# Score products moved ahead in the early slots, two maxima per even slot at the hand-over, and a new order of the tail, in a kernel of threshold attention followed by a gated two-layer product

## The chip, the cores and the metric

The kernel runs on one core of one Trainium2 chip. A core has five engines that work at the same time, each in the order of its own queue: TensorE (PE, matrix products and transposes through the array), VectorE (DVE), ScalarE (ACT), GpSimd (POOL) and SyncE (SP, which here only starts DMAs). The metric is the time of one execution in device microseconds; lower is better.

## What is computed

Eight batches of eight heads, 576 positions, head dimension 64. Scores within tau of the row's maximum stay, all others are dropped; what is left goes through a softmax and is multiplied with v. The result, as 4608 tokens of 512 features, goes through two products with an activation between them.

```python
scores = scale * np.matmul(q, k.transpose(0, 1, 3, 2))
thresh = np.max(scores, axis=-1, keepdims=True) - tau
scores = np.where(scores >= thresh, scores, -1000000000.0)
scores = scores - np.max(scores, axis=-1, keepdims=True)
attn = np.exp(scores)
attn = attn / (np.sum(attn, axis=-1, keepdims=True) + 1e-09)
return np.matmul(attn, v).astype(np.float32)
...
h = x @ w_in
relu6 = np.clip(h + 3.0, 0.0, 6.0)
g = h * relu6 / 6.0
return (g @ w_out).astype(np.float32)
```

## The kernel before

**Slots.** Four heads make a quad (two pairs), and a quad has nine slots. Slots 0 to 3 are the four blocks of 128 query rows of the first pair, 4 to 7 those of the second, and slot 8 takes the 64 rows left over of both pairs. A slot holds the scores of two heads, 128 rows by 576 keys each. There are 16 quads and so 144 slots, which one loop goes through (L518); `now` is the number of the slot in hand. The order of the instructions on every engine is written out by hand, and there is no scheduler: an engine does what its queue says in the order in which the loop recorded it.

**One slot's way through the engines.** `scores(n)` (L287, PE) writes the scores to PSUM. `sm_max` (L302, DVE) copies them to the tile `s` and takes the row maximum of each head; its last line (L305, POOL) makes the bias from it. `sm_mask` (L309, ACT) rejects what is below the threshold, `sm_exp` (L314, ACT) takes the exponential and the row sum. `sm_recip` (L317, DVE) inverts the sum, `sm_norm` (L322, POOL) multiplies and writes `pn` in bf16, to be transposed into `pT` (or `pR` for slot 8): for most slots up to 20 by PE (`pe_transpose`, L337, and a DVE copy L338), for all others by a DMA that SP starts (L330). In iteration n the loop takes the maxima of slot n+1, the mask and exp around slot n, the norm of slot n-1, the transposition of slot n-2, and the scores of slot n+2.

**Products.** `products` says after which slot `av_main` (L346, L349) multiplies pT with v into `xT`, and `av_rest` does so with pR into `xR`. The DVE copies them out of PSUM (L357, L367).

**q and k.** They have to be transposed: for the first two batches by PE (L232, L257, L259; `turns` says in which slot) with a copy by DVE or ACT (L239, L220, L222, L265), later by DVE itself. `loads` are closures that start the loads of q and k, on SP for the first two batches and partly on POOL (kr) later; one or none is started in each slot. `casts` and `vcasts` do the same for the weights and for v, on POOL.

**The two layers.** An item of `todo1` is one first-layer product: `mm1` (L381, or L376 for the odd tokens, the 64 rows of slot 8 in two batches), the activation `mm1_relu` (on ACT in even slots, L389, on DVE in odd ones, L391) and the gate `mm1_gate` (L404, DVE). Items of the odd tokens write their gate to `go`, of which there is one buffer, and a DMA transposes it into `g` (L406). A token tile of `todo2` is the second-layer product of 128 tokens, 16 matmuls in four pieces (`mm2_part`, L415), and `mm2_out` (L421 on ACT, L423 on DVE) copies it out for the final DMA. There are no items before slot 22 (`N1`); from there each slot takes one item, and two pieces of a tile go into every even slot once there are tiles.

**PSUM.** It has eight banks. Scores take banks 0, 1, 3 and 4 (in odd slots after 24 another set of columns, reaching into 2 and 5), transposes and products take turns in 2 and 5 (`bank()`), bank 6 (`HB`) holds PE's transposed pn, dummy transposes and the items, bank 7 (`OB`) the token tile or an item.

**Dummy transposes.** `warm_up(6)` puts six transposes of the identity on PE in each of the first eight slots.

**Tail.** After the loop come the last products, the items left over, the norm of the last slot, the first eight items of the last batch (`head`), the rest of the products (`av_rest` needs pR of slot 143), the tiles in hand, then the twelve last items (`tail`), and the last three tiles. In the tail items take banks 0, 1, 3 and 4 in turn, tiles take banks 7 and 6.

Of the kernel before, what the change touches and what calls it, by code (L numbers as in the profile page):

```python
# [20 lines left out]
def kernel(  # L21
# [17 lines left out]
    NQUAD = B * H // 4  # L39
    NSLOT = 9  # L40
    NB = 2
    N1 = 22
    N2 = 28
    HB, OB = 6, 7
# [171 lines left out]


    def copy_out(out, in_):
        if 0 <= now < N1:
            nc.vector.tensor_copy(out=out, in_=in_)  # L220
        else:
            nc.scalar.copy(out=out, in_=in_)  # L222
# [54 lines left out]
    def scores(n):  # L277
        quad, slot = divmod(n, NSLOT)
        w0 = 320 if first(n) else 384
        for k0, w in ((0, w0), (w0, S - w0)):  # L280
            for i in range(2 if slot == 8 else 1):
                for a in range(2):
                    pair = 2 * quad + (i if slot == 8 else slot // 4)
                    rows = slice(64 * i, 64 * i + 64) if slot == 8 else slice(0, P)
                    q0 = 512 if slot == 8 else slot % 4 * P
                    c0, kc = score_col(n, a) + k0, 64 * (1 - a) + k0
                    nc.tensor.matmul(ps_flat[rows, c0:c0 + w],  # L287
                                     qT_of(pair)[a * 64:(a + 1) * 64, q0:q0 + rows.stop - rows.start],
                                     kT_of(pair)[a * 64:(a + 1) * 64, kc:kc + w], start=True, stop=True)
# [4 lines left out]
    def sm_max(sl):  # L294
        sl.s = s_pool.tile([P, 2, S], F32, tag="s", name="s")
        sl.m = stat_pool.tile([P, 2], F32, tag="m", name="m")
        sl.bias = stat_pool.tile([P, 2], F32, tag="bias", name="bias")
        sl.rsum = stat_pool.tile([P, 2], F32, tag="rsum", name="rsum")
        sl.rinv = stat_pool.tile([P, 2], F32, tag="rinv", name="rinv")
        for i in range(2):  # L300
            c0 = score_col(sl.n, i)
            nc.vector.tensor_scalar(out=sl.s[:, i, :], in0=ps_flat[:, c0:c0 + S],  # L302
                                    scalar1=1.0, scalar2=None, op0=Alu.mult, op1=Alu.max,
                                    accum_out=sl.m[:, i:i + 1])
        nc.gpsimd.tensor_scalar(out=sl.bias[:], in0=sl.m[:], scalar1=-scale, scalar2=tau, op0=Alu.mult, op1=Alu.add)  # L305

    def sm_mask(sl, i):
# [8 lines left out]
    def sm_recip(sl):  # L316
        nc.vector.reciprocal(out=sl.rinv[:], in_=sl.rsum[:])  # L317
# [122 lines left out]
    def moe_of(b):  # L440
        items = []
        for c0, mts in (((0, (5, 6)), (None, (4,)), (256, (7, 8))) if b % 2 else ((0, (0, 1)), (256, (2, 3)))):
            for ni in range(0, NI, 4 if c0 is None else 2):
                items.append(((b, ni, c0), ()))
            items[-1] = (items[-1][0], [(b // 2, mt, part) for mt in mts for part in range(4)])
        if b % 2:
            items[10:14] = items[12:14] + items[10:12]
        return items[0:8], items[8:]

    alloc_qk(0)  # L450
# [24 lines left out]
            queue.append(sl)  # L475
    scores(0)
    sm_max(queue[0])
    scores(1)

    turns = {1: [("q", 1)], 2: [("k", 1)], 3: [("rest", 0)]}  # L480

    def turn_at(n, job, of):
        turns.setdefault(n, []).append((job, of))

    for quad in range(1, NQUAD):
        n0 = quad * NSLOT
        first_odd = n0 - 9 + quad % 2
        for i, (job, of) in enumerate((("q", 2 * quad), ("k", 2 * quad), ("rest", quad),
                                       ("q", 2 * quad + 1), ("k", 2 * quad + 1))):
            turn_at(n0 + (-5, -4, -3, 0, 1)[i] if quad < 3 else  # L490
                    first_odd + (0, 2, 3, 4, 6)[i] if quad > 3 else first_odd + (0, 2, 3, 5, 7)[i], job, of)

    products = {}
    for quad in range(NQUAD):
        p0, p1 = 2 * quad, 2 * quad + 1
        if quad < NB:
            jobs = ((8, p0, 0, 512), (12, p1, 0, 512), (13, None, 0, 0))
        else:
            jobs = [(7 - quad % 2 + 2 * i, *of) for i, of in enumerate(
                ((p0, 0, 256), (p0, 256, 256), (p1, 0, 256), (p1, 256, 256), (None, 0, 0)))]  # L500
        for after, *of in jobs:
            products.setdefault(quad * NSLOT + after, []).append((quad, *of))

    def multiply(n):
# [6 lines left out]
                todo1.extend(moe_of(of // 2)[0])  # L511
        return copies

    prev = None
    last_keys = []
    part = 0
    waiting = []
    for n, sl in enumerate(queue):  # L518
        quad, slot = sl.quad, sl.slot
        b, g = divmod(quad, 2)  # L520
        now = n
        if slot in (0, 4):
            pts[2 * quad + slot // 4] = pt_pool.tile([P, 9, 512], BF16, tag="pT", name="pT")
        if slot == 8:
            ptr[quad] = ptr_pool.tile([P, 9, P], BF16, tag="pR", name="pR")
        for ahead in {0: (1, 2), 9: (3,), 16: (4,)}.get(n, (quad + 2,) if quad > 2 and slot == (2 if quad == 3 else 0) else ()):
            if ahead < NQUAD:
                load_quad(ahead)
        if slot == 0 and g == 1 and b + 1 < B:
            load_v(b + 1)  # L530
        for copy in last_keys:
            copy()
        last_keys = []
        if 0 < n <= N1:
            for i in range(2):
                sm_exp(prev, i)
        if n + 1 < len(queue):
            sm_max(queue[n + 1])
        even = n >= N1 and n % 2 == 0
        if n > N1:  # L540
            sm_recip(prev)
        for copy in waiting:
            copy()
        waiting = []

        if todo1:
            item, then = todo1.pop(0)
            h = mm1(item, OB if n > N1 and n % 2 and not pieces else HB)
            todo2.extend(then)
        else:  # L550
            item = None
        if n >= N1:
            for copy in multiply(n):
                copy()
        if item:
            mm1_gate(item, h, mm1_relu(h, on_act=even))
        copies = pe_transpose(queue[n - 2]) if n > 1 and queue[n - 2].on_chip else None
        if prev is not None and n < N1:
            sm_recip(prev)
        if copies:  # L560
            copies()
        pieces = 2 if n % 2 == 0 and todo2 else 0
        for _ in range(pieces):
            bb, mt, part = todo2.pop(0)
            mm2_part(bb, mt, part)
        if n <= N1:
            for i in range(2):
                sm_mask(sl, i)
        if n == N1:
            sm_recip(prev)  # L570
        if n >= N1:
            for i in range(2):
                sm_exp(sl, i)
            if n + 1 < len(queue):
                for i in range(2):
                    sm_mask(queue[n + 1], i)
        if n < N1:
            for copy in multiply(n):
                copy()
        if part == 3:  # L580
            waiting.append(lambda tile=(bb, mt): late.extend(mm2_out(*tile, on_act=False)))
            part = 0
        evict = []
        for job, of in turns.get(n, ()):
            if job == "k":
                (last_keys if even else evict).append(transpose_k(of))
            elif job == "q":
                if of // 2 not in qkT:
                    alloc_qk(of // 2)
                (waiting if even else evict).append(transpose_q(of))  # L590
            else:
                (last_keys if even else evict).append(transpose_rest(of, of_k=of > 0))
        for out_of_psum in evict:
            if out_of_psum:
                out_of_psum()
        if n == 0:
            warm_up(8)
        if n <= N1:
            scores(n + 2)
        elif n % 2:  # L600
            for m in (n + 3, n + 2):
                if m < len(queue):
                    scores(m)
        if n < 8:
            warm_up(6)
        if n > 0:
            sm_norm(prev)
        flush()
        if n == 0:
            start(loads, 2)  # L610
        elif n not in (4, 12, 15, 18, 21) and not 23 < n < 30 and (n < 37 or n % 2 == 0):
            start(loads, 1)
        if n < 4 or 15 < n < 20 or n > 33:
            start(vcasts, 1 if n < N1 or n % 2 else 0)
        else:
            start(casts, 2 if n in (5, 8, 11, 14) or 21 < n < 28 else 1)
        prev = sl
# [34 lines left out]
    sm_recip(prev)  # L652
    sm_norm(prev)
    head, tail = moe_of(B - 1)
    for item in head:
        rest1(*item)
    av_main(2 * last + 1, 256, 256)()
    av_rest(last)()
    rest2()
# [38 lines left out]
```

## Time and profile before

| what | value |
|---|---|
| median of 13 runs | 522.2 us (521.39 to 524.29) |
| the profiled execution | 522.2 us |
| its span, first to last instruction | 520.4 us |
| granted clock of TensorE | 1.00 |
| busy: PE, ACT, DVE, POOL | 506.3, 452.0, 442.4, 299.3 us |

```profile
L309 ACT ACTIVATE s<-s,bias 128x576 f32<-128x576 f32 x288 | 205.9, 763 | 6.0 <-POOL bias L305 5.7
L314 ACT ACTIVATE s<-s 128x576 f32<-128x576 f32 x288 | 192.6, 671 | 0.3
L287 PE MATMUL ps<-kT,qT 64*128 64x384 f32 (+7 forms) x1280 | 174.0, 419 | 4.7 <-DVE s L302 3.8
```

A row of the page's costliest groups names the line, the engine and the operation, what it writes and reads, how often, then the busy time and the mean length of one in ns, then how long the engine stood idle ahead of it and what ended most of that. The whole execution falls into a start, slots 0 to 21 with attention alone (to about 76 us), slots 22 to 143 with both (to about 468 us), and the tail. An engine's share of the whole span says little about any of these, so the readings below go by stage.

### The profile page before, as it was taken

To read this page: it belongs to the slowest core of one execution; us is meant where nothing else is said; L and a number is where in the kernel's file an instruction comes from. 1 tells how busy PE (TensorE), PEld (TensorE's weight loads), DVE (VectorE), ACT (ScalarE), POOL (GpSimd) and SP (SyncE) were. 2 spreads that over 40 slices of the span, in tenths; PEclk is the share of its full clock that TensorE was granted. 3 is DMA by queue.
4 is the path that set the end of the run, shared out by engine and by line. 5 is a ranking of instruction groups with operands and counts; after the bars stand their busy time and mean duration, and the time that the engine had idled before them with its cause. 6 is when DMAs were issued, how large, how long until landed. Compare 5 with 4: busy or idle time off the path is not lost.

```text
span 520.4 us, 12124 instructions
## 1 busy us (share of the span) xinstructions
PE 506.3 (97%) x4145; PEld 321.4 (62%) x4145; DVE 442.4 (85%) x1124; ACT 452.0 (87%) x980; POOL 299.3 (58%) x538
## 2 busy tenths in 40 slices
PE   8999999999999999999999999999999999999997
PEld 6765556666665666666665666666655666667463
DVE  3788887998999999999999999999999999878151
ACT  3999979999999989999999999999999999995060
POOL 1778869756676655657566656657566655551000
PEclk9999999999999999999999999999999999999999
DMA  5899899989899999999989999999999996574222
GB/s 131 118 174 166 143 158 143 195 142 170 153 167 180 164 179 167 175 162 170 175 160 173 172 184 160 160 172 171 159 157 189 181 172 113 112 112 70 83 61 60
DMA packets 314094, 78.77 MB, mean 151 GB/s; under 512 B 296624, under 2 KB 309168, under 8 KB 314032
## 3 DMA queue, kind: packets, MB, share of 16 engines
q1 hardware_dynamic: 294464, 67.90, 77.0%
q0 software_dynamic: 18368, 9.71, 15.1%
q8 instruction: 32, 0.52, 0.4%
q10 hardware_dynamic: 1200, 0.39, 0.3%
q14 instruction: 30, 0.25, 0.1%
HBM read 36.70 MB, written 9.44 MB: 89 GB/s over the span
## 4 chain that ended last, share of the span: by engine, by line
PE 76%; ACT 3%; DMA 2%; DVE 2%; issue 1%; POOL 1%; POOLq 0%; DVEq 0%
PE ps L287 24%; PE ps L415 23%; PE ps L381 19%; PE ps L346 6%; PE ps L376 2%; ACT s L309 1%; PE ps L349 1%; ACT s L314 1%; DMA pT<-pn 1%; ACT r L389 1%; DVE s L302 1%; DMA pR<-pn 1%; POOL pn L322 1%; DVE g L404 1%; DMA g<-go 1%
## 5 line engine op out<-in xcount | busy, mean ns | idle before, releaser
L322 POOL TENSOR_SCALAR pn<-s,rinv 128x576 bf16<-128x576 f32 x288 | 210.6, 743 | 18.7 <-issue 4.4
L302 DVE TENSOR_SCALAR_CACHE_REDUCE s<-ps 128x576 f32<-128x576 f32 x288 | 205.1, 749 | 17.5 <-PE ps L287 9.0
L309 ACT ACTIVATE s<-s,bias 128x576 f32<-128x576 f32 x288 | 205.9, 763 | 6.0 <-POOL bias L305 5.7
L314 ACT ACTIVATE s<-s 128x576 f32<-128x576 f32 x288 | 192.6, 671 | 0.3
L287 PE MATMUL ps<-kT,qT 64*128 64x384 f32 (+7 forms) x1280 | 174.0, 419 | 4.7 <-DVE s L302 3.8
L287 PEld LDWEIGHTS ps<-kT,qT 64*128 64x128 f32 (+1 forms) x1280 | 103.6, 175 | 59.3 <-issue 15.8
L415 PE MATMUL ps<-w_out_sb,g 128*128 128x512 bf16 x576 | 134.0, 379 | 0.0
L381 PE MATMUL ps<-xT,w_in_sb 128*128 128x256 bf16 x1024 | 130.8, 273 | 1.2 <-DVE g L404 0.7
L381 PEld LDWEIGHTS <-w_in_sb 128*128 128x128 bf16 x1024 | 95.5, 98 | 41.0 <-issue 22.2
L305 POOL TENSOR_SCALAR bias<-m 128x2 f32<-128x2 f32 x144 | 26.9, 187 | 155.6 <-DVE rinv L317 138.7
L404 DVE SCALAR_TENSOR_TENSOR g<-r,ps 128x512 bf16<-128x512 f32 x128 | 87.6, 687 | 9.6 <-ACT r L389 5.6
L415 PEld LDWEIGHTS <-g 128*128 128x128 bf16 x576 | 56.3, 98 | 56.6
L389 ACT ACTIVATE r<-ps,three 128x512 f32<-128x512 f32 x81 | 55.4, 687 | 29.4 <-PE ps L381 21.8
L314 ACT ACTIVATION_READ_ACCUMULATOR s<-s 128x1 f32 x288 | 54.6, 190 | 0.0
L391 DVE TENSOR_SCALAR r<-ps 128x512 f32<-128x512 f32 x63 | 42.9, 681 | 0.0
L346 PE MATMUL ps<-pT,vm 128*64 128x256 bf16 (+1 forms) x480 | 39.1, 285 | 0.5 <-DMA pT<-pn 0.5
L346 PEld LDWEIGHTS <-vm 128*64 128x64 bf16 x736 | 27.2, 110 | 17.0 <-issue 14.8
L357 DVE CAST xT<-ps 128x256 bf16<-128x256 f32 (+1 forms) x60 | 26.3, 438 | 13.2 <-PE ps L349 13.2
L423 DVE TENSOR_SCALAR osb<-ps 128x512 f32<-128x512 f32 x31 | 20.9, 673 | 13.1 <-PE ps L415 13.1
L302 DVE DVE_READ_ACCUMULATOR s<-ps 128x1 f32 x288 | 23.9, 83 | 0.0
L317 DVE RECIPROCAL rinv<-rsum 128x2 f32<-128x2 f32 x144 | 23.0, 160 | 0.6 <-ACT s L314 0.6
L143 POOL DMA_DIRECT2D vm<-in_v_dram x28 | 21.4, 765 | 0.7 <-issue 0.7
(57 smaller groups left out, 259.9 us busy)
## 6 DMA issues: line engine op xcount, KB each, us to landing
out_dram<-osb SPq DMA_DIRECT2D x31, 256.0 KB, 3.0
nq<-in_q_dram SPq DMA_DIRECT2D x96, 72.0 KB, 3.7
km<-in_k_dram SPq DMA_DIRECT2D x96, 64.0 KB, 3.2
vm<-in_v_dram POOLq DMA_DIRECT2D x24, 128.0 KB, 4.4
km<-in_k_dram SPq DMA_DIRECT2D x16, 128.0 KB, 4.2
w_in_sb<-in_moe_w_in_dram POOLq DMA_DIRECT2D x16, 128.0 KB, 3.9
w_out_sb<-in_moe_w_out_dram POOLq DMA_DIRECT2D x16, 128.0 KB, 4.8
pT<-pn SPq DMA_TRANSPOSE x117, 4.1
```

The costliest lines, as they stand in the source:

```text
L287: nc.tensor.matmul(ps_flat[rows, c0:c0 + w], qT_of(pair)[a * 64:(a + 1) * 64, q0:q0 + rows.stop - rows.start], kT_of(pair)[a * 64:(a + 1) ...
L302: nc.vector.tensor_scalar(out=sl.s[:, i, :], in0=ps_flat[:, c0:c0 + S], scalar1=1.0, scalar2=None, op0=Alu.mult, op1=Alu.max, accum_out=sl ...
L305: nc.gpsimd.tensor_scalar(out=sl.bias[:], in0=sl.m[:], scalar1=-scale, scalar2=tau, op0=Alu.mult, op1=Alu.add)
L309: nc.scalar.activation(out=s, in_=s, func=Act.Prelu, bias=sl.bias[:, i:i + 1], scale=scale, alpha=REJECT)
L314: nc.scalar.activation(out=s, in_=s, func=Act.Exp, accum_out=sl.rsum[:, i:i + 1])
L322: nc.gpsimd.tensor_scalar(out=pn[:, i, :], in0=sl.s[:, i, :], scalar1=sl.rinv[:, i:i + 1], scalar2=1.0, op0=Alu.mult, op1=Alu.mult)
L346: nc.tensor.matmul(pb[a * 64:(a + 1) * 64, :], vm[:, 2 * hp + a, c * D:(c + 1) * D], pT[:, 5 * a + c, cols], start=(c == 0), stop=False)
L381: nc.tensor.matmul(ps[:, hb, n * 256:(n + 1) * 256], w_in_sb[:, ki, (ni + n) * P:(ni + n + 1) * P], xT[b][:, ki, c0:c0 + 256], start=(ki = ...
L389: nc.scalar.activation(out=r, in_=hps, func=Act.Relu, bias=three[:])
L391: nc.vector.tensor_scalar(out=r, in0=hps, scalar1=3.0, scalar2=0.0, op0=Alu.add, op1=Alu.max)
L404: nc.vector.scalar_tensor_tensor(out=out, in0=r, scalar=6.0, in1=hps, op0=Alu.min, op1=Alu.mult)
L415: nc.tensor.matmul(o_ps[0], gbuf[:, ni, mt * P:(mt + 1) * P], w_out_sb[:, ni, :], start=(ni == 0), stop=(ni == NI - 1))
```

## The change

It has two parts.

**The tail.** The odd tokens' second two items of the last batch come after four other items instead of after two (`items[10:16]`). In slot 142 the two pieces of the token tile are recorded ahead of the item's product. The item of slot 143 uses bank 0. After the loop, the tiles in hand are taken between the seventh and the eighth item of `head`, ahead of the last products.

**The slots up to 28.** In slots 3 to 22 (`N0` to `N1`) `scores(n + 2)` is recorded right after the maxima and the reciprocal, ahead of PE's transposes and products; the copies of these are kept in `waiting` and recorded in the next slot, behind its maxima and its reciprocal. The slots in which q and k of quads 1 and 2 are transposed, and in which products of quads 0 and 1 are taken, are moved, five loads instead of two are started in slot 0, and dummy transposes are left in slots 0, 1, 2, 3 and 6. The bias is a function of its own (`sm_bias`). In the even slots from 22 to 28 the maxima of slots n+1 and n+2 are both taken, ahead of the item's gate, and none in the odd slots between. There exp comes ahead of the item's activation, and in slot 22 both masks (22 and 23) do too.

```diff
--- before.py
+++ after.py
@@ -39,6 +39,7 @@
     NQUAD = B * H // 4
     NSLOT = 9
     NB = 2
+    N0 = 3
     N1 = 22
     N2 = 28
     HB, OB = 6, 7
@@ -216,7 +217,7 @@
 
 
     def copy_out(out, in_):
-        if 0 <= now < N1:
+        if 0 <= now <= N1:
             nc.vector.tensor_copy(out=out, in_=in_)
         else:
             nc.scalar.copy(out=out, in_=in_)
@@ -302,6 +303,8 @@
             nc.vector.tensor_scalar(out=sl.s[:, i, :], in0=ps_flat[:, c0:c0 + S],
                                     scalar1=1.0, scalar2=None, op0=Alu.mult, op1=Alu.max,
                                     accum_out=sl.m[:, i:i + 1])
+
+    def sm_bias(sl):
         nc.gpsimd.tensor_scalar(out=sl.bias[:], in0=sl.m[:], scalar1=-scale, scalar2=tau, op0=Alu.mult, op1=Alu.add)
 
     def sm_mask(sl, i):
@@ -443,8 +446,10 @@
             for ni in range(0, NI, 4 if c0 is None else 2):
                 items.append(((b, ni, c0), ()))
             items[-1] = (items[-1][0], [(b // 2, mt, part) for mt in mts for part in range(4)])
-        if b % 2:
+        if b % 2 and b < B - 1:
             items[10:14] = items[12:14] + items[10:12]
+        elif b % 2:
+            items[10:16] = items[12:16] + items[10:12]
         return items[0:8], items[8:]
 
     alloc_qk(0)
@@ -475,6 +480,7 @@
             queue.append(sl)
     scores(0)
     sm_max(queue[0])
+    sm_bias(queue[0])
     scores(1)
 
     turns = {1: [("q", 1)], 2: [("k", 1)], 3: [("rest", 0)]}
@@ -487,14 +493,14 @@
         first_odd = n0 - 9 + quad % 2
         for i, (job, of) in enumerate((("q", 2 * quad), ("k", 2 * quad), ("rest", quad),
                                        ("q", 2 * quad + 1), ("k", 2 * quad + 1))):
-            turn_at(n0 + (-5, -4, -3, 0, 1)[i] if quad < 3 else
+            turn_at(n0 + ((-5, -5, -4, -2, -1) if quad == 1 else (-6, -5, -4, -2, -1))[i] if quad < 3 else
                     first_odd + (0, 2, 3, 4, 6)[i] if quad > 3 else first_odd + (0, 2, 3, 5, 7)[i], job, of)
 
     products = {}
     for quad in range(NQUAD):
         p0, p1 = 2 * quad, 2 * quad + 1
         if quad < NB:
-            jobs = ((8, p0, 0, 512), (12, p1, 0, 512), (13, None, 0, 0))
+            jobs = ((8, p0, 0, 512), (13 - 2 * quad, p1, 0, 512), (15 - 3 * quad, None, 0, 0))
         else:
             jobs = [(7 - quad % 2 + 2 * i, *of) for i, of in enumerate(
                 ((p0, 0, 256), (p0, 256, 256), (p1, 0, 256), (p1, 256, 256), (None, 0, 0)))]
@@ -511,9 +517,16 @@
                 todo1.extend(moe_of(of // 2)[0])
         return copies
 
+    def second():
+        nonlocal pieces, bb, mt, part
+        pieces = 2 if now % 2 == 0 and todo2 else 0
+        for _ in range(pieces):
+            bb, mt, part = todo2.pop(0)
+            mm2_part(bb, mt, part)
+
     prev = None
     last_keys = []
-    part = 0
+    pieces = bb = mt = part = 0
     waiting = []
     for n, sl in enumerate(queue):
         quad, slot = sl.quad, sl.slot
@@ -535,17 +548,37 @@
             for i in range(2):
                 sm_exp(prev, i)
         if n + 1 < len(queue):
-            sm_max(queue[n + 1])
+            if n <= N1 or n > N2 + 1 or n % 2 == 0:
+                sm_max(queue[n + 1])
+            sm_bias(queue[n + 1])
         even = n >= N1 and n % 2 == 0
-        if n > N1:
+        if n >= N0:
             sm_recip(prev)
         for copy in waiting:
             copy()
         waiting = []
-
-        if todo1:
+        if N0 <= n <= N1:
+            scores(n + 2)
+            if n in (3, 6):
+                warm_up(6)
+        if even and n <= N2:
+            sm_max(queue[n + 2])
+        if n == N1:
+            for i in range(2):
+                sm_mask(sl, i)
+        exp_first = even and n <= N2
+        if exp_first:
+            for i in range(2):
+                sm_exp(sl, i)
+        if n == N1:
+            for i in range(2):
+                sm_mask(queue[n + 1], i)
+
+        if todo1 and n >= N1:
             item, then = todo1.pop(0)
-            h = mm1(item, OB if n > N1 and n % 2 and not pieces else HB)
+            if n == len(queue) - 2:
+                second()
+            h = mm1(item, 0 if n == len(queue) - 1 else OB if n > N1 and n % 2 and not pieces else HB)
             todo2.extend(then)
         else:
             item = None
@@ -554,29 +587,27 @@
                 copy()
         if item:
             mm1_gate(item, h, mm1_relu(h, on_act=even))
-        copies = pe_transpose(queue[n - 2]) if n > 1 and queue[n - 2].on_chip else None
-        if prev is not None and n < N1:
+        if n > 1 and queue[n - 2].on_chip:
+            waiting.append(pe_transpose(queue[n - 2]))
+        if prev is not None and n < N0:
             sm_recip(prev)
-        if copies:
-            copies()
-        pieces = 2 if n % 2 == 0 and todo2 else 0
-        for _ in range(pieces):
-            bb, mt, part = todo2.pop(0)
-            mm2_part(bb, mt, part)
-        if n <= N1:
+            for copy in waiting:
+                copy()
+            waiting = []
+        if n != len(queue) - 2:
+            second()
+        if n < N1:
             for i in range(2):
                 sm_mask(sl, i)
-        if n == N1:
-            sm_recip(prev)
         if n >= N1:
-            for i in range(2):
-                sm_exp(sl, i)
-            if n + 1 < len(queue):
+            if not exp_first:
+                for i in range(2):
+                    sm_exp(sl, i)
+            if n != N1 and n + 1 < len(queue):
                 for i in range(2):
                     sm_mask(queue[n + 1], i)
         if n < N1:
-            for copy in multiply(n):
-                copy()
+            waiting.extend(multiply(n))
         if part == 3:
             waiting.append(lambda tile=(bb, mt): late.extend(mm2_out(*tile, on_act=False)))
             part = 0
@@ -590,24 +621,26 @@
                 (waiting if even else evict).append(transpose_q(of))
             else:
                 (last_keys if even else evict).append(transpose_rest(of, of_k=of > 0))
+        evict = [out_of_psum for out_of_psum in evict if out_of_psum]
+        if N0 <= n < N1:
+            waiting.extend(evict)
+            evict = []
         for out_of_psum in evict:
-            if out_of_psum:
-                out_of_psum()
+            out_of_psum()
         if n == 0:
             warm_up(8)
-        if n <= N1:
+        if n < N0:
             scores(n + 2)
-        elif n % 2:
+            warm_up(6)
+        elif n > N1 and n % 2:
             for m in (n + 3, n + 2):
                 if m < len(queue):
                     scores(m)
-        if n < 8:
-            warm_up(6)
         if n > 0:
             sm_norm(prev)
         flush()
         if n == 0:
-            start(loads, 2)
+            start(loads, 5)
         elif n not in (4, 12, 15, 18, 21) and not 23 < n < 30 and (n < 37 or n % 2 == 0):
             start(loads, 1)
         if n < 4 or 15 < n < 20 or n > 33:
@@ -652,8 +685,10 @@
     sm_recip(prev)
     sm_norm(prev)
     head, tail = moe_of(B - 1)
-    for item in head:
+    for item in head[0:7]:
         rest1(*item)
+    rest2()
+    rest1(*head[7])
     av_main(2 * last + 1, 256, 256)()
     av_rest(last)()
     rest2()
```

## The prediction

> **What bounds the kernel now.** I read the page's busy shares first, then busy time by stage, then the waits of each engine, then the timeline. The profiled execution took 522.2 us, of which the span is 520.4; the median of the 13 runs is 522.2 too, so a sum made on the span may be taken off the median.
>
> ```profile
> PE 506.3 (97%) x4145; PEld 321.4 (62%) x4145; DVE 442.4 (85%) x1124; ACT 452.0 (87%) x980; POOL 299.3 (58%) x538
> 21.46:70.12 48.66, 45.79 (x375) 29.22 (x374) 41.97 (x117) 46.39 (x103) 39.70 (x72) 1.00 1.03 167
> 70.12:76.12 6.00, 5.73 (x51) 3.31 (x51) 4.78 (x12) 2.77 (x6) 4.19 (x7) 1.00 0.90 112
> 80.70:102.46 21.76, 19.60 (x154) 13.79 (x152) 18.63 (x49) 21.67 (x49) 18.78 (x35) 1.00 1.28 184
> 102.46:458.90 356.44, 355.96 (x2992) 223.43 (x2990) 333.60 (x850) 336.82 (x741) 218.87 (x388) 1.00 1.02 164
> ```
>
> In the rows by stage the figures are length, then busy time of PE, PE loads, DVE, ACT, POOL, then clock. From 102.5 to 458.9 us PE is the bound (355.96 of 356.44). From 80.7 to 102.5 it is ACT (21.67 of 21.76). Slots 4 to 21 (21.46 to 70.12) are ACT's as well, nearly: it is idle for 2.27 us. Then, in slot 22, it stands still for 3.2 us:
>
> ```profile
> ACT s L309 <- POOL bias L305: 2.3, 5, 0.6
> ACT r L389 <- PE ps L381: 3.2, 1, 3.2
> 75.03 1.05 PE L381 MATMUL ps<-xT,w_in_sb 128*128 128x256 bf16 x8
> 76.12 0.69 ACT L389 ACTIVATE r<-ps,three 128x512 f32<-128x512 f32 x1 [3.23 <-PE ps L381]
> 76.70 1.43 ACT L309 ACTIVATE s<-s,bias 128x576 f32<-128x576 f32 x2
> ```
>
> ACT's first hidden-layer activation sits in its queue ahead of slot 22's mask, and waits for a projection that PE reaches only after scores(23). The third place is the end, where PE waits:
>
> ```profile
> PE ps L381 <- DVE g L404: 0.7, 1, 0.7
> PE ps L381 <- DVE go L404: 0.6, 1, 0.6
> PE ps L346 <- DMA pR<-pn: 0.3, 1, 0.3
> ```
>
> The steady stage is not touched by the diff, so all that can change lies before 102.5 and after 458.9. Work saved in the first part arrives at the end in full, because PE then starts its 356 us earlier.
>
> **What the Trainium skill says.** "Perfetto Trace Analysis", section "Tensor Engine Instruction", says that ACT, DVE and GpSimd work strictly in the order of their queues and that the end of a matmul is modelled. The 3.23 us wait agrees: slot 22's bias was ready at 72.6 us (POOL wrote it at 72.45) and its mask stood behind the activation until 76.7. "TensorE: Matmul & The Clock Gate", section "What's actually happening", says that TensorE falls to half its clock after an idle window of about 3.4 us. No stage of the trace shows it: slots 8 to 21 have no dummy transposes, and the granted clock is 1.00 in all of them.
>
> **The change part by part.**
>
> Slots 3 to 21. Moved: scores(n+2) goes ahead of PE's pn transposes, products and q/k transposes, and the copies of these go behind the maxima of the next slot. Nothing is added; the same instructions run. The question is what the cycle costs each engine. ACT: two exps and two masks; mask starts at 15.64 and 18.30, 24.14 and 26.81 give 2.67 us a slot without a wait. Seventeen slots are 45.4 us, against 48.66 now, so 3.3 us is the most to gain (2.27 by the busy column, whose overlapping durations hide small gaps).
>
> DVE and PE: the maxima need scores, scores need the maxima before them to be through.
>
> ```profile
> 10.99 0.76 DVE L302 TENSOR_SCALAR_CACHE_REDUCE s<-ps 128x576 f32<-128x576 f32 x1 [1.02 <-PE ps L287]
> 13.49 0.76 DVE L302 TENSOR_SCALAR_CACHE_REDUCE s<-ps 128x576 f32<-128x576 f32 x1 [1.05 <-PE ps L287]
> 26.39 0.74 DVE L338 COPY pT<-ps 128x1152 bf16<-128x1152 bf16 x1
> 27.05 0.68 DVE L220 COPY kT<-ps 128x512 f32<-128x512 f32 x1
> 28.05 0.76 DVE L302 TENSOR_SCALAR_CACHE_REDUCE s<-ps 128x576 f32<-128x576 f32 x1 [0.32 <-issue]
> ```
>
> The first two rows, 2.50 us apart, are that cycle with no copies. With copies DVE needs 1.36 for two maxima, 0.07 for the reciprocal, 0.66 for a pT copy, about 0.68 for a q, k or xT copy, 0.86 for the three small ones of a rest. The third to fifth rows show such a slot, and 0.32 us lost at its end since the scores came after the copies. With scores first, a slot costs the larger of 2.50 and 1.43 plus its copies. By the new order, slots 4 to 20 have: 2.50, 2.79, 2.95, 2.50, 2.77, 2.80, 2.50, 2.50, 2.50, 2.77, 2.80, 2.95, 2.50, 2.77, 2.80, 2.50, 2.77. The sum is 45.7, and it runs ahead of or behind ACT's 2.67 by at most 0.4 us on the way. So DVE and ACT are now equal, and ACT loses some 0.4 us more. A PE slot with a product (scores to 1.2 us after the maxima, product 1.43, q or k transposes 0.6, sum 3.2) is late by 0.5 us, but the slot after it has 1.37 us of copies ahead of the next maxima, which hides it. Gain between 0 (any 0.2 us more in each DVE slot takes it all) and 2.9; I take 2.6.
>
> POOL: bias 0.2, two norms 1.47, weight loads 0.57 or 1.12 make 2.3 to 2.85 us a slot; slots 5, 8, 11, 14 have the 2.85, within what DVE gives. The loads of quad 1 all start in slot 0: three more closures, four pairs of DMAs of some 1.25 us each on SP, 5.0 us. SP is free from 9.8 us and its first transposing DMA is issued at 16.80, so they fit, and quad 1's data is there by slot 4 (they land in 3 to 4 us). Quad 4's last load comes in slot 20 instead of 22: 1.28 us more on POOL there, which holds bias(22) back by about 0.8. Three of the eight sets of dummy transposes after slot 3 go: nothing, since PE has real work there; if the clock did fall to half, slots 4 to 7 would need some 4.8 us instead of 2.67, 8.5 us in all.
>
> Slot 22. On ACT, mask(22), exp(22) and mask(23) now stand ahead of the activation: three pairs, 4.0 us, which need only bias(22) and max(23). max(23) no longer waits for copies of its own slot. The 3.23 us go. What is late next is the same activation: PE does scores(24) (1.24) once max(23) ends, 2.4 us after exp(21), then the projection (1.05); with latencies and PE's leftover work the activation can start 4.95 us after exp(21). ACT is there at 4.0, and held back by bias(22) at 4.8, both inside the same wait. 0.95 is given back: gain 2.3, between 1.3 and 3.2.
>
> Slots 23 to 28. Both maxima of a pair of slots are now taken in the even one, ahead of the gate, and exp goes ahead of the activation. ACT is already 99.6% busy here with the same instructions, so nothing to gain by itself: 0. Below: the gate of an even slot stands behind max(n+2), which waits for scores(n+2). I place the gate of slot 22 at 6.2 us after exp(21), and PE wants that bank for slot 24 at 8.7, a margin of 2.5. Above: PE is idle 2.16 us in this stage, and scores that are released sooner could let it enter the steady stage with a longer lead, up to 1.5.
>
> Loop end. In slot 142 two pieces of the token tile (1.73 us) go ahead of the projection, which waited 0.66 for a gate. The projection and its activation come 1.05 later, ACT's exp(142) with them, and recip(142), which stands ahead of the xT copy on DVE, ends at 468.6, where that copy started before. So DVE keeps its absolute times, and PE, 0.66 earlier, meets them four banks later: gate of the second leftover item at 473.4, wanted at 473.0. Of 0.66 I count 0.1.
>
> Tail. The leftover tiles (ten pieces, 8.7 us) go between the seventh and eighth items of the last batch and so ahead of the products with pR: its 0.28 us wait goes, covered by 8.7. The second pair of odd items comes six after the first: the first transposing DMA took 3.5 us with its wait, four items of 0.9 us now lie in it, so the 0.57 goes. The second transposition lands about 12.0 us after the tail's start, and is wanted at 12.3: nothing, with 0.3 to spare. 0.85 together.
>
> Sum: 2.6 + 2.3 + 0 + 0.1 + 0.85 = 5.85, so 522.2 - 5.85 = 516.4 (rounded up).
>
> **The rivals.**
>
> DVE's cycle doesn't shorten. The scores come sooner, but reciprocal, late copies and reads of PSUM keep slots at 2.8 us; for it speaks that my DVE sum equals ACT's. Then only slot 22 and the end remain: 2.3 + 0.95 = 3.25, 519.0.
>
> The lead counts. PE's idle 2.16 us in slots 23 to 28 shrinks too, by 1.5: 514.9. For it speaks that PE's long matmul rows there (2.88 against 2.2 us in the steady stage) contain waits; against it, that ACT is full.
>
> Slower: the gate behind the second maxima. In slots 22, 24, 26 and 28 DVE stands at max(n+2) until PE has done scores(n+2), the gate is late, its bank holds the projection two slots on, and ACT's activation waits with all masks behind it. It decides from a lateness of 2.5 us on. At 1.9 us lost by ACT in each of four slots, 7.6: 516.4 + 7.6 = 524.0; below 1.46 each the change is still a gain.
>
> **How the numbers follow.** Forecast 0.55 (515.4 to 517.8), DVE's cycle 0.20 (517.8 to 521), the lead 0.15 (513.6 to 515.4), the gates 0.10. The range 514.4 to 519.8 leaves out the slower case and the ends of two others. About 0.2%, 1 us, is what this kernel's runs can tell from no change: faster 0.86, no change 0.05, slower 0.09.
>
> **What would show it.** ACT's wait for the first activation falls from 3.2 to about 1 us; that activation stands after slot 23's mask; the masks of slots 4 to 21 are 2.7 us apart; the steady stage begins near 97.5 instead of 102.5 and is as long as before; the waits for pR and go are absent. The prediction is wrong if masks stay 2.85 apart, if new waits of ACT appear between slots 22 and 30, or if PE's clock drops below 1.00 before slot 8.

## The result, and the profile after

The changed kernel took 517.0 us (median of 7 runs, 516.42 to 517.45) against 522.31 us before (32 runs); the ratio is 0.9894 with a 95% interval of 0.9882 to 0.9907. The prediction said 516.4. The profiled execution has a span of 514.8 us, 5.6 us less than before.

These are rows of busy time by stage, of the changed kernel, in the columns used before (length, then busy time of PE, PE loads, DVE, ACT, POOL, then clock, DMA share and GB/s). The stages end at the mask of slot 21, at ACT's copies of k in slot 23, at the first piece of a token tile, and at the activation of slot 140.

```profile
21.30:67.94 46.64, 45.04 (x355) 27.59 (x355) 40.78 (x115) 45.95 (x103) 39.78 (x73) 1.00 1.07 163
67.94:77.26 9.32, 9.32 (x101) 6.25 (x101) 8.80 (x25) 7.55 (x17) 8.22 (x15) 1.00 0.94 142
77.26:97.60 20.34, 19.51 (x162) 12.91 (x155) 18.35 (x48) 20.28 (x47) 17.33 (x32) 1.00 1.02 172
97.60:454.63 357.03, 356.42 (x2993) 223.37 (x2991) 334.77 (x853) 337.99 (x741) 219.21 (x389) 1.00 1.06 164
```

The second row is the hand-over, in which ACT still stands idle for 1.77 us; in the others ACT, and then PE, is nearly full. Taking the same five points from both timelines gives where the time came from:

| stretch, in the profiled executions | before, us | after, us | less | predicted |
|---|---|---|---|---|
| start to the mask of slot 4 | 21.46 | 21.30 | 0.16 | 0 |
| to the mask of slot 21 | 48.66 | 46.64 | 2.02 | 2.6 |
| to ACT's copies of k in slot 23 | 10.58 | 9.32 | 1.26 | 2.3 |
| to the activation of slot 140 | 378.19 | 377.37 | 0.82 | 0 |
| to the start of the last copy out of PSUM | 58.15 | 56.76 | 1.39 | 0.95 |

The sum is 5.65, where the medians differ by 5.3. The waits of ACT up to 110 us in the changed kernel, and those of PE after 450 us, are these (who waits, for what, us in total, times, longest):

```profile
ACT s L312 <- POOL bias L308: 4.7, 4, 3.3
ACT kT L223 <- DVE qT L266: 1.0, 1, 1.0
```

```profile
PE ps L384 <- DVE g L407: 0.2, 1, 0.2
```

The wait for the first activation, 3.2 us, is gone from ACT's list, and pR and go are gone from PE's. Of the 4.7 us, 3.3 is the start of the kernel, as before. But a wait that nobody had on the list has come: ACT's copies of k behind a copy of q on DVE. The timeline of ACT in slots 22 and 23 of the changed kernel (start, us, engine, line, operation; idle before it and releaser in brackets) shows it beside a second one:

```profile
71.39 1.44 ACT L312 ACTIVATE s<-s,bias 128x576 f32<-128x576 f32 x2 [0.69 <-POOL bias L308]
74.07 1.43 ACT L312 ACTIVATE s<-s,bias 128x576 f32<-128x576 f32 x2
75.61 0.69 ACT L392 ACTIVATE r<-ps,three 128x512 f32<-128x512 f32 x1
77.26 0.53 ACT L223 COPY kT<-ps 64x128 f32<-64x128 f32 x2 [0.96 <-DVE qT L266]
```

The order is as the change has it: both masks, then the activation, which now waits for nothing that is named. The mask of slot 22 waits 0.69 us for its bias, and after the activation ACT loses 0.96 us more. Up to the end of the activation, 0.96 us before those copies, the hand-over had gained 2.22 us: by then ACT has done what took it 10.58 us before, and it took 8.36.

### The profile page after: what moved, and what is told of

Same layout as the page of the kernel before. It is cut to its first block, busy times and chain, and to the rows that moved or that the text cites. A ratio compares the mean times of both kernels' runs of the same rounds, so it can differ in the third digit from the quotient of the medians.

```text
span 514.8 us, 12094 instructions
## 1 busy us (share of the span) xinstructions
PE 504.5 (98%) x4127; PEld 318.3 (62%) x4127; DVE 442.0 (86%) x1124; ACT 451.8 (88%) x980; POOL 299.3 (58%) x538
## 4 chain that ended last, share of the span: by engine, by line
PE 79%; ACT 5%; DVE 2%; issue 0%
PE ps L288 24%; PE ps L418 24%; PE ps L384 20%; PE ps L349 7%; PE ps L379 3%; ACT s L317 2%; ACT s L312 2%; PE ps L352 1%; ACT r L392 1%; DVE g L407 1%; DVE r L394 0%; PE ps L340 0%; DVE s L303 0%; ACT kT L223 0%; PE ps L258 0%
```

## The experiments

The experiments fall into four groups, each on a chip of its own with the kernel before beside it: the first four below, then the next three and the last one (slot 142 back), then the table of three, then the repetition of one kernel. The medians of the kernel before were 522.0, 522.06, 522.31 and 522.48 us in these groups. As they differ by up to 0.5 us, kernels of different groups are better compared by their ratios to the kernel before. "Start-corrected" below means counted from the mask of slot 4.

**The tail alone.** The kernel before, with the diff's lines on `items[10:16]`, `second()` in slot 142, bank 0 for slot 143, and:

```diff
-    for item in head:
+    for item in head[0:7]:
         rest1(*item)
+    rest2()
+    rest1(*head[7])
     av_main(2 * last + 1, 256, 256)()
```

> The kernel before with the four edits of the tail alone. Theory (the three parts add up, and the end gives what the two traces show behind slot 140, 1.3 us): 522.3 - 1.3 = 521.0, waits for pR and go absent, PE 0.5 us ahead after slot 142's move. Rival (the prediction's sizes: 0.1 + 0.85): 521.35. Rival (the end's gain needs the early part, since DVE's times there are absolute): no change, 522.3.

520.5 us, ratio 0.9968 (0.9956 to 0.9980): 1.5 us. From slot 140's activation to the last copy its profile has 56.76 us, to the hundredth what the whole change has there. So the end's gain is its own, needs nothing of the early part, and is 1.4, not 0.95. Between the copies of k and slot 140, where this kernel's code is that of before, its profile has 377.86 us against 378.19: so 0.33 of the table's 0.82 is no more than two executions differ by.

**The tail and slots 3 to 21, the old hand-over.** The changed kernel with slots 22 to 28 in the old order:

```diff
-            if n <= N1 or n > N2 + 1 or n % 2 == 0:
-                sm_max(queue[n + 1])
+            sm_max(queue[n + 1])
...
-        if N0 <= n <= N1:
+        if N0 <= n < N1:
             scores(n + 2)
...
-        exp_first = even and n <= N2
+        exp_first = False
...
-        if n < N1:
+        if n <= N1:
             for i in range(2):
                 sm_mask(sl, i)
```

> The changed kernel with the old order in slots 22 to 28, so slots 3 to 21 and the tail are as changed. Theory: 2.0 us from slots 4 to 20 reach the end in full, 521.0 - 2.0 = 519.0, mask of slot 21 near 67.9 us, and the first activation again holds ACT up for about 3 us in slot 22. Rival (that stall of slot 22 swallows what the slots gain, because PE's first projection has its own time): 521.0, stall of 5 us.

519.4 us, ratio 0.9948 (0.9934 to 0.9962), between the two sizes expected. Two expectations stood against each other here, that the slots' gain reaches the end and that slot 22 swallows it. The mask of slot 21 is 46.65 us after that of slot 4, so the slots gave their 2.0; but ACT's copies of k came only 0.79 us sooner than with the tail alone (start-corrected 58.45 against 59.24). This wait of ACT took the difference:

```profile
ACT r L392 <- PE ps L384: 4.5, 1, 4.5
```

It was 3.2 and is now 4.5. The rival was right in kind: while ACT's queue holds the activation ahead of slot 22's mask, PE's projection sets the time and more than half of what the slots gain is lost there. The hand-over's own part is then the rest: 2.4 us by the medians (519.4 to 517.0), 2.8 by the ratios, and 2.49 by the traces, up to the copies of k.

This kernel also bears on the table's 0.82. From the copies of k to the activation of slot 140 it has 377.46 us, with slots 22 to 28 in the old order, where the changed kernel has 377.37. So what is left of the 0.82 does not come from the new order of those slots; what it comes from is not shown.

**Both maxima early in slot 22 alone.**

```diff
-    N2 = 28
+    N2 = 22
```

> The changed kernel with the two maxima per even slot and exp first in slot 22 alone; slots 24 to 28 in the old order. Theory (the ramp is ACT's, full in both orders): 517.0 +- 0.4. Rival (the lead counts: taking both maxima early in 24 to 28 gave 0.4 to 0.8 us): 517.6. Rival (the gate behind the second maxima costs): 516.4 or less.

517.21 us, ratio 0.9902 (0.9886 to 0.9918); the changed kernel's median is inside its runs. The first token tile starts 1.28 us later than in the changed kernel (start-corrected 77.58 against 76.30; 98.77 against 97.60 as the traces have it), yet the last copy only 0.26 later (start-corrected). These are PE's waits from 76 to 110 us, in this kernel and then the longest in the changed one, which has three more of 0.2 or 0.3 us:

```profile
PE ps L288 <- DVE s L303: 1.8, 3, 1.0
```

```profile
PE ps L384 <- DVE g L407: 0.6, 1, 0.6
```

The early maxima take the long waits for DVE away and put PE 1.3 us ahead, but most of that is paid back. The gate that PE waits for at 100.25 us is that of slot 30, which has no second maxima. These are its activation and the gate itself in the changed kernel:

```profile
98.80 0.68 ACT L392 ACTIVATE r<-ps,three 128x512 f32<-128x512 f32 x1
99.51 0.69 DVE L407 SCALAR_TENSOR_TENSOR g<-r,ps 128x512 bf16<-128x512 f32 x1
```

The maxima and the reciprocal ahead of it on DVE are through at 99.38, and the activation at 99.48. So it is ACT, full in this stage (20.28 of 20.34 us), that takes 0.6 of the lead back. For the rest no wait is named. In these two executions the lead counts for 0.26, and no wait for a gate behind the second maxima shows.

**The product slots.** Slots 4 to 20 gave 2.0 and were predicted to give 2.6. The timeline shows the slots one by one. This is DVE around slot 9, and PE from slot 8's product to the scores recorded in slot 9, in the changed kernel:

```profile
35.72 0.75 DVE L303 TENSOR_SCALAR_CACHE_REDUCE s<-ps 128x576 f32<-128x576 f32 x1
37.14 0.67 DVE L360 CAST xT<-ps 128x512 bf16<-128x512 f32 x1
37.73 0.68 DVE L221 COPY kT<-ps 128x512 f32<-128x512 f32 x1
38.83 0.76 DVE L303 TENSOR_SCALAR_CACHE_REDUCE s<-ps 128x576 f32<-128x576 f32 x1 [0.42 <-POOL pn L325]
```

```profile
35.69 1.05 PE L349 MATMUL ps<-pT,vm 128*64 128x512 bf16 x8
36.58 0.38 PE L352 MATMUL ps<-pT,vr 128*64 128x512 bf16 x2
36.89 0.66 PE L233 MATMUL ps<-identf,km 128*128 128x128 f32 x4
37.48 1.24 PE L288 MATMUL ps<-kT,qT 64*128 64x384 f32 x8
```

From one first maximum to the next it is 3.11 us, where the prediction had 2.80: the copies end at 38.4, but the scores, behind the product and the transposes, end at 38.7. The releaser named is POOL's, which had long been done; the scores are what came last. Slots 14 and 18 show the same 3.11. The edit moves the transposes out of the slots with a product:

```diff
-            turn_at(n0 + ((-5, -5, -4, -2, -1) if quad == 1 else (-6, -5, -4, -2, -1))[i] if quad < 3 else
+            turn_at(n0 + ((-5, -5, -4, -3, -2) if quad == 1 else (-7, -6, -4, -3, -2))[i] if quad < 3 else
```

> The changed kernel with the q and k transposes of quads 1 and 2 moved out of the slots that have a product of 512 columns (8, 13, 17), one slot earlier or two. Theory (what slots 4 to 20 lack to ACT's own pace is PE's lateness behind product and transposes, 0.42 us in slots 9, 14 and 18): maxima in these slots 2.5 to 2.7 us apart instead of 3.11, mask of slot 21 about 0.8 us earlier, 516.2. Rival (POOL's weight loads in slots 5, 8, 11, 14 set the pace): mask of slot 21 unchanged at 67.9, 517.0.

515.05 us, ratio 0.9865 (0.9847 to 0.9883): by the medians 2 us less than the changed kernel, by the ratios 1.5. This is DVE around slot 9 in this kernel, and then the stage from the mask of slot 4 to that of slot 21:

```profile
35.74 0.75 DVE L303 TENSOR_SCALAR_CACHE_REDUCE s<-ps 128x576 f32<-128x576 f32 x1
37.17 0.67 DVE L360 CAST xT<-ps 128x512 bf16<-128x512 f32 x1
38.27 0.76 DVE L303 TENSOR_SCALAR_CACHE_REDUCE s<-ps 128x576 f32<-128x576 f32 x1 [0.43 <-issue]
```

```profile
21.32:67.04 45.72, 45.65 (x360) 29.12 (x358) 41.37 (x116) 45.51 (x102) 40.60 (x74) 1.00 1.08 166
```

Slot 9 is 2.53 us. The seventeen slots take 45.72 us, 2.69 each, and from slot 7 on the masks are 2.66 to 2.68 apart, which is ACT's own pace. The expected 0.8 came as 0.92, and 0.67 more in slot 22, because DVE and POOL are no longer late when they get there: the mask of slot 22 waits 0.1 us instead of 0.69. The two make 1.6, which agrees with the ratios. POOL's double weight loads, the rival, are still in their slots and hold nothing up.

**The hand-over's two waits.** Quad 3's transposes are moved to slots in which DVE, not ACT, makes the copies, and quad 4's last load goes back to slot 22.

```diff
-                    first_odd + (0, 2, 3, 4, 6)[i] if quad > 3 else first_odd + (0, 2, 3, 5, 7)[i], job, of)
+                    first_odd + (0, 2, 3, 4, 6)[i] if quad > 3 else first_odd + (-1, 0, 2, 5, 7)[i], job, of)
...
-        elif n not in (4, 12, 15, 18, 21) and not 23 < n < 30 and (n < 37 or n % 2 == 0):
+        elif n not in (4, 12, 15, 18, 20, 21) and not 23 < n < 30 and (n < 37 or n % 2 == 0):
```

> The changed kernel with quad 3's transposes of slots 19, 21 and 22 in 18, 19 and 21, and quad 4's last load in slot 22 as it was before the change. Theory (the entry gave 1.3 instead of 2.3 because bias(22) stood behind that load on POOL, 0.69 us, and ACT's copies of k behind a q copy that DVE had behind the gate, 0.96): both waits of ACT go, a wait of some 0.8 us for the first activation comes in their place, and ACT's first exp of slot 23 starts 1.0 to 1.8 us sooner: 515.2 to 516.0. Rival (PE's first projection sets the hand-over and the waits only share its time): 516.8 or more.

What was expected came at the place and not at the end. Both waits are gone; the activation waits 0.54 us and the mask of slot 23 0.37 us for its bias; and slot 23's exp starts at 76.32 instead of 77.81 us. But the median is 517.06 us (514.94 to 518.77, ratio 0.9901, 0.9881 to 0.9922), no better than the changed kernel. PE's waits between 102 and 454 us, where the changed kernel has none:

```profile
PE ps L349 <- DMA pT<-pn: 2.1, 1, 2.1
```

It is one product, at 180 us, that waits for a transposed tile, in a stretch whose code is the same. From slot 23's exp to the activation of slot 140 this execution has 379.02 us against 376.82, so the wait took what the hand-over had gained. The other five executions were not profiled. Together with the product slots:

> The product slots of the run before and the entry together. Theory (ACT's own pace to slot 22, then a hand-over without its copies of k): 1.3 to 1.5 us less than the product slots alone, 513.6 to 513.8. Rival (at ACT's pace PE or DVE is the next to be late in slot 22): within 0.4 of the product slots alone, 514.7 to 515.4.

514.73 us (514.13 to 516.27, ratio 0.9867, 0.9851 to 0.9883): the early gain again, and 2.3 us of waits for pT in two places. Without the dummy transposes of slots 3 and 6 on top:

```diff
-            if n in (3, 6):
-                warm_up(6)
```

> As both together, without the dummy transposes of slots 3 and 6. Theory (they delay the scores of slots 5 and 8, and slot 4 was 2.88 us long instead of 2.50): masks 5 to 7 2.67 us apart instead of 2.84 and 2.89, 0.3 to 0.4 us less than both together, clock 1.00. Rival (they hold the clock up): a clock below 1.00 before slot 10, and 2 us or more lost.

514.54 us (513.83 to 514.9, ratio 0.9857, 0.9844 to 0.9870), which cannot be told from the kernel with them. In the trace it can: the masks of slots 5, 6 and 7 are 2.66 and 2.74 apart instead of 2.84 and 2.90, which is 0.34 us, and the clock stays at 1.00. PE waits 1.2 us for pT, by the times at the same two products as in the run before (at 119 and 178 us).

**Which edit brings the waits for pT?** Three kernels, all with the product slots and without those dummies: nothing more; with quad 3's transposes moved; with quad 4's load moved.

> The product slots and no dummy transposes after slot 2; the entry as in the changed kernel. Theory (the dummies cost 0.35 us): 514.7, no wait of PE for pT between 102 and 454 us, times within 0.6 us of each other.

> As the run before, and quad 3's transposes moved out of slot 22; quad 4's load stays in slot 20. Theory (the entry's edit puts PE about 1 us further ahead of ACT at the hand-over, and PE gives that back at transposing DMAs that land as late as before): PE waits 1 to 2 us for pT somewhere in 102 to 454 us, 514.3 to 515. Rival (the load moved to slot 22 brought those waits): none of them, 513.3 to 513.6.

> As the first of these three, and quad 4's last load in slot 22; quad 3's transposes as in the changed kernel. Theory (PE's lead): no wait for pT, 514.5 to 514.9. Rival (the moved load): waits for pT of 1 to 2 us, 515.5 or more, times spread over more than 1 us.

| kernel | us | ratio to before | PE waits for pT |
|---|---|---|---|
| neither | 514.79 (514.49 to 515.83) | 0.9852 (0.9828 to 0.9877) | none |
| quad 3's transposes moved | 513.52 (513.3 to 513.95) | 0.9828 (0.9803 to 0.9852) | none |
| quad 4's load moved | 514.84 (514.76 to 515.86) | 0.9857 (0.9832 to 0.9882) | none |

Neither edit alone brings them. The theory of the second kernel, that PE's lead costs waits, fails there, and its rival, that the moved load does, fails in the third. Within this group, moving quad 3's transposes is worth 1.27 us. The kernel with both was then run once more, unchanged:

> The kernel with product slots, no dummies, quad 3's transposes moved and quad 4's load in slot 22, once more. Theory (the two last edits together bring PE's waits for pT): waits of 1 to 2 us between 102 and 454 us again, times spread over more than 0.8 us, 514.3 to 514.9. Rival (they were chance): no such wait, 513.3 to 513.7 as with the load in slot 20.

513.7 us (513.09 to 514.87, ratio 0.9835, 0.9821 to 0.9849), and no wait for pT in its profile. So the two edits do not bring the waits by themselves: the same program had 1.2 us of them in one profiled execution and none in another, on another chip. Nor do they need the edits: the kernel before has one such wait, 0.48 us at 190 us, and the kernel with the tail alone one of 0.18. But the three kernels with more than 1 us all have both edits and all ran on one chip, where the changed kernel with slot 142 back, which has neither edit, showed none. Chance and a property of that chip are not told apart.

The traces do show where the delay arises. These are the two transpositions that SP starts ahead of the product at 178 us, in the first execution of this kernel and in the second (start and length of SP's work):

```profile
174.14 2.76 SPq L333 DMA_TRANSPOSE pT<-pn  x2
169.88 3.55 SPq L333 DMA_TRANSPOSE pT<-pn  x2
```

POOL writes pn at the same times in both (it begins one at 164.26 and at 164.13 us, the next at 168.87 and at 168.73), but SP starts these DMAs 4.3 us later in the first. From start to landing they take no longer there (3.3 to 4.5 us against 3.3 to 5.5, for those between 165 and 181 us). So it is SP that was behind. From 152 us on its rows follow one another without a gap in both, and their lengths differ: the transposition into g just ahead of these two, for one, took 2.87 us instead of 1.24. So a lag of 0.95 us at 152 us grew to 4.3. Why SP's rows took longer stays open.

The second of the three kernels has the lowest median of all, 513.52 us (ratio 0.9828), against 517.0 (0.9894) for the change; the repeated kernel, at 0.9835, cannot be told from it. This is ACT in slots 22 and 23 of it:

```profile
70.14 1.44 ACT L312 ACTIVATE s<-s,bias 128x576 f32<-128x576 f32 x2
74.37 0.69 ACT L392 ACTIVATE r<-ps,three 128x512 f32<-128x512 f32 x1
74.96 0.67 ACT L317 ACTIVATE s<-s 128x576 f32<-128x576 f32 x1
```

Exp follows on the activation; there are no copies of k and no wait between them.

**Slot 142 back.** The changed kernel, with the token tile's pieces of slot 142 behind the projection again:

```diff
-            if n == len(queue) - 2:
-                second()
...
-        if n != len(queue) - 2:
-            second()
+        second()
```

> The changed kernel with slot 142's projection ahead of its token tile again. Prediction's size (DVE keeps its absolute times, so the move is worth 0.1 us): 517.1, and from slot 140's activation to the last copy 56.9 us. Rival (it is worth most of the wait of 0.66 us): 517.5, 57.2 to 57.4 us. The other two waits of the tail stay absent in both.

516.67 us (516.56 to 517.1, ratio 0.9899, 0.9884 to 0.9913), which cannot be told from the changed kernel. From slot 140's activation to the last copy it is 56.95 us instead of 56.76. PE's wait after 440 us is back, and it is nearly all free:

```profile
PE ps L384 <- DVE g L407: 0.7, 1, 0.7
```

Removing a wait of 0.7 us brought 0.19, as the prediction's argument said: DVE keeps its times, and PE meets it some items later, where the changed kernel shows the 0.2 us of waiting seen above.

## Why the prediction was right, and where it was off

The direction and the total were right (5.3 us by the medians, 5.85 forecast), and each part's mechanism was seen to work: the tail's in a kernel of its own, the slots' and the hand-over's by taking the hand-over back. The terms were not equally good, and their errors partly cancel. Slots 3 to 22 gave 1.6 us less than forecast, the end 0.4 more; and 0.98 us of the table's sum lies in the two stretches for which nothing was forecast. That the total came so near is in part luck. Of the named signs of being wrong one did appear, a new wait of ACT between slots 22 and 30.

- Slots 3 to 21: the cycle of scores and maxima did shorten, and the first rival (it doesn't) falls. Of the seventeen slot lengths listed, thirteen are within 0.16 us of what the changed kernel shows. The step that failed is the sentence that a product slot's lateness of 0.5 us is hidden by the next slot's copies: slots 9, 14 and 18 are 3.11 us long instead of 2.80, 0.9 in all, and the experiment with moved transposes took 0.92 away. Slot 4 was 2.88 instead of 2.50; without the dummies the masks that follow it are near ACT's pace (2.66 and 2.74).
- Slot 22: the stall of 3.2 us went. Up to the end of the activation the forecast of 2.3 holds (2.22), though not by the route forecast: the prediction put the late bias(22) inside a wait for the activation, and it was the bias that ACT waited for, 0.69, and not the activation. The step that failed is that the sum stops there. It leaves out the copy of q on DVE, queued behind the gate, for which ACT's copies of k then wait 0.96, so that 1.26 arrives. With quad 3's transposes moved, where ACT is spared the wait and the copies too, 1.27 us came back. The skill's page "PSUM — Partial Sum Buffer", section "PSUM bank collisions raise a hardware error", says that two engines, ACT and DVE reading among them, must not be in the same bank and the same group of 32 partitions at once, even at different addresses. The two copies read different columns of the same partitions of one bank, and ACT's starts 0.04 us after DVE's ends, which agrees. No run put the two into different banks, so that the bank is the reason is not shown by itself.
- "Arrives at the end in full" was too simple: with the old hand-over only 0.8 of the slots' 2.0 us got past slot 22. With the new one it holds, which is how the prediction used it: the 1.6 us that the moved transposes gain up to the copies of k are there at the end of the span too (513.2 against 514.8).
- Slots 23 to 28: 0 was right within 0.26. The second rival (the lead counts) falls, as 1.3 us of lead became 0.26; the slower rival (the gate behind the maxima) falls too, as no such wait shows.
- Loop end and tail: 0.1 for slot 142 was right (0.19). The rest was taken for 0.85 and is 1.20. The idle time shown was the term: the stretch of the last twelve items and three tiles got 0.73 shorter for a wait of 0.57, and the stretch before it, from slot 140's activation, 0.48 for a wait of 0.28 beside those 0.19. The starts of PE's rows in the kernel before tell why:

```profile
496.62 1.91 PE L381 MATMUL ps<-xT,w_in_sb 128*128 128x256 bf16 x16
498.37 1.89 PE L376 MATMUL ps<-w_in_sb,xR 128*128 128x512 bf16 x8
500.10 1.91 PE L381 MATMUL ps<-xT,w_in_sb 128*128 128x256 bf16 x16
502.57 3.65 PE L381 MATMUL ps<-xT,w_in_sb 128*128 128x256 bf16 x32 [0.57 <-DVE go L404]
```

  A row of two items is listed with 1.91 us, but the next one starts 1.75 after it. From 500.10 to 502.57 that leaves 0.72 and not 0.57. In the same way the products with pT and pR start 0.56 us apart with the wait for pR and 0.10 apart without it, so that this wait was worth 0.46 and not 0.28. The listed ends reach into the wait and hide a part of it.
- The clock: dummy transposes go without loss. The runs without those of slots 3 and 6 keep 1.00 and are not slower, in line with the section "What's actually happening" of "TensorE: Matmul & The Clock Gate" named in the prediction, as PE has no idle window of that length: the longest idle time listed from 9.5 to 34 us in such a run is 0.87 us.

## What to carry to other kernels

When two engines alternate, write the length of every slot as the larger of the chain and each engine's queue, and do not let one slot's queue hide another's unless both ends are computed: three slots of 0.3 us each were missed that way. Where a stage hands over to another, look at what the queue of the bounding engine holds first, because time gained ahead of such a place can be lost in it; and follow its queue past the instruction that was held up, to the next one that needs another engine. A copy on one engine can wait for a copy on another although they touch different columns and different results, as ACT's copies of k did here; the wait went when both were given to one engine. To price a wait of PE, take the starts of the rows around it and compare them with the same rows where nothing waits: two waits listed with 0.57 and 0.28 us were worth 0.73 and 0.48.

## What was not expected of the hardware

SP, which only starts DMAs, can be several us behind in one execution and not in another. The same kernel, with an unchanged order, had PE wait 1.2 us for tiles to be transposed in one profiled execution, where SP started a transposition 4.3 us later, and not at all in another, on another chip. Kernels with the same code between 102 and 454 us had between nothing and 2.3 us of such waits.
